# ScalarE issues 30 of the 93 SBUF-to-SBUF copies that SyncE issued, one group later

## The chip, the cores and the metric

One Trainium2 chip, one of its cores. The metric is the device time of one execution in microseconds (us), as the median of several. Engines are named as in the profile: PE (TensorE, with PEld for its weight loads), DVE (VectorE), ACT (ScalarE), POOL (GpSimd) and SP (SyncE), which issues transfers. A row that names `SPq` is SP's queue of instructions.

## What is computed

Two steps over x of 4 batches, 12608 positions and 128 channels:

```python
# 1: a gated long convolution
u = x * v
y = irfft(rfft(u, n=2*S) * rfft(h_filt, n=2*S)[None], n=2*S)[:, :S]   # along the positions
x = x * y
# 2: an expert on the 128 best-scored rows of each batch
scores = x @ w_gate
for b in range(B):
    top_idx = the 128 largest scores of the batch
    xe = x[b, top_idx]
    out[b, top_idx] = xe + sigmoid(scores[b, top_idx])[:, None] * (relu(xe @ w1) @ w2)
```

## The kernel before, in words

The convolution is done by Hartley transforms that are split into a transform over 93 and one over 250 points. The 128 channels are cut into 32 groups of four, so the main loop (line 1249) runs over 128 groups `t`, 32 for each of the 4 batches. In one turn of the loop a new group goes forward: `f_s1` and `dft` on PE, copies on ACT (L483, L344), the product with the filter on DVE (`f_u`, `f_v`, `f_y`: L487 to L501), and a sum and a difference on POOL (`f_sd`: L508, L509). In the same turn the inverse transform `f_i` (L546) runs for a group three turns back, and ACT copies its results out of PSUM (L550 and L551, a pair of copies for two of the four channels). `stage_u` on POOL (L324) multiplies x and v of a group three turns ahead.

PE works in strips of 32 rows, three of which a group needs. The fourth strip is used for every fourth group: the groups with t % 4 = 1, 2, 3 each compute one third of group t - t % 4 in their rows 96 to 127. So three groups of four have a finishing step: POOL adds and subtracts the last columns (`f_c`, L589, two instructions), and then `put(k)` (L559 to L562) moves the third from partitions 96 to 127 of group k to the partitions of group t - t % 4, by a transfer from SBUF to SBUF of 126 KB. There are 93 puts, 84 of them of the whole width. Of the last three groups of batches 0 to 2, ACT copies most of the columns itself (L582) and the put takes the rest.

When all groups of a batch are through (turn 34 of the loop for batch 0, then every 32 turns), `P1.run` does the second inverse step: PE (L636) reads `ay`, the results of all 32 groups, and so has to wait for the puts. DVE multiplies with x (L647), and the scores are summed on ACT (L701). The search for the 128 best rows of a batch runs in small steps in the turns of the next batch.

All transfers of the loop are issued by SP in the order in which the program writes them, and each waits on SP until what it needs is ready: x and v of a group four turns ahead (`load_u`, L318), the stores of the filter's spectrum to DRAM in the first batch (L1305) and its loads in the others (L330), the puts, and the rows of x for `P1` (L611). At the end of a turn stands the list of puts: `due` holds the groups that the turn before finished, and their puts are issued then, one turn after `f_c` was written.

The order on each engine is that of the program (`manual_schedule`). On ACT the end of a turn lies behind the second of the two L483 copies; what follows are the L550 and L551 copies of the next turn, one pair or two, and then L344.

Of the kernel before, what the change touches and what calls it, by code (L numbers as in the profile page):

```python
# [23 lines left out]
NG = 32  # L24
# [214 lines left out]
def hyena_moe(ctx, tc, xg, x2, pos, bw, ww, wg, mw1, mw2, cs, c1, gx, cf, ci, wm, tk, out):  # L239
    nc = tc.nc  # L240
# [73 lines left out]
    def load_u(t):  # L314
        b = t // NG
        if b < B:
            for k, n in enumerate("xv"):
                nc.sync.dma_start(buf(n, t, [NP, XC]), xg[b, :, GC[t], k])  # L318

    def stage_u(t):  # L320
        if t >= B * NG:
            return
        x, v = buf("x", t, [NP, XC]), buf("v", t, [NP, XC])
        nc.gpsimd.tensor_tensor(out=x, in0=x, in1=v, op=ALU.mult)  # L324
# [13 lines left out]
    def dft(t, te, pq):  # L338
        for w in (1, 0):
            for a in range(0, 128, 32):  # L340
                nc.tensor.matmul(pq[w][a:a + 32], lhsT=cf_sb[:, 2 * w + a // NQ, a % NQ:a % NQ + 32],  # L341
                                 rhs=te[:, a // NQ], start=True, stop=True)
        qs = buf("qs", t, [128, HC])
        nc.scalar.copy(out=qs, in_=pq[1])  # L344
        return qs
# [129 lines left out]
    def f_s1(t, dst=None, ps=bank1):  # L475
        u = buf("x", t, [NP, 4, N3])
        te = buf("te", t, [128, 2, 4, N1]) if dst is None else dst
        tps = [view(ps[h], 0, [128, 2, 2, N1]) for h in range(2)]
        for s in range(4):
            for k, c in enumerate(BLK):  # L480
                nc.tensor.matmul(tps[s // 2][c, s % 2], lhsT=u[:, s, c], rhs=c1_sb[:, k], start=True, stop=True)  # L481
        for h in range(2):
            nc.scalar.copy(out=te[:, :, 2 * h:2 * h + 2].rearrange("p e s i -> p s e i"), in_=tps[h])  # L483
        return te.rearrange("p e s i -> p e (s i)")

    def f_u(pq, qs):
        nc.vector.tensor_tensor(out=nat(pq[0]), in0=nat(pq[0]), in1=rev(qs), op=ALU.add)  # L487

    def f_v(pq, qs):
        nc.vector.tensor_tensor(out=nat(pq[1]), in0=rev(pq[0]), in1=nat(qs), op=ALU.subtract)  # L490

    def f_y(t, uv):
        ht = buf("ht", HI[t], [128, 2, HC]) if HS[t] != "hh" else hh[:, GC[t]].rearrange("p e s i -> p e (s i)")
        mt, yz = buf("mt", t, [128, 2, HC]), buf("yz", t, [128, 2, HC])
        for e in (1, 0):
            for o, k in ((mt[:, e], 0), (uv[e], 1)):
                nc.vector.tensor_tensor(out=o, in0=uv[e], in1=ht[:, k], op=ALU.mult)  # L497
        yield yz
        nc.vector.tensor_tensor(out=yz[:, 0], in0=uv[1], in1=mt[:, 0], op=ALU.add)  # L499
        yield yz  # L500
        nc.vector.tensor_tensor(out=yz[:, 1], in0=mt[:, 1], in1=uv[0], op=ALU.subtract)  # L501
        yield yz
# [50 lines left out]
    def parts(t, cols):  # L553
        k = t % 4 - 1
        i, o = ay[96:, GC[t]], ay[32 * k:32 * k + 32, GC[t - t % 4]]
        i, o = (x.rearrange("p (e j) s -> p e (j s)", e=2)[:, :, 4 * cols[0]:4 * cols[1]] for x in (i, o))
        return o, i

    def put(t, *cols):  # L559

        o, i = parts(t, cols or (0, NJ))
        nc.sync.dma_start(o, i)  # L562

    def turn(i):

        g, r = i % NG, i % 4
        if i > DIR:
            u = [(t, s) for t in ((i, DIR) if i == DIR + 1 else (i,)) for s in range(4)]
        elif r == 0:
            u = [(i - 1, s) for s in (1, 2, 3)] if g else []  # L570
        else:
            u = {1: [(i, 0), (i, 1), (i, 2)], 2: [(i - 1, 3), (i, 0), (i, 1)], 3: [(i - 1, 2), (i - 1, 3), (i, 0)]}[r]
            if g == NG - 1:
                u += [(i, s) for s in (1, 2, 3)]
        done = []
        for t, s in u:
            f_i(t, s)
            if s == 3:
                done.append(t)
                if t % NG >= NG - 3 and t < DIR:  # L580
                    o, i = parts(t, (0, JM))
                    nc.scalar.copy(out=o, in_=i)  # L582
        return done

    def f_c(t, ops=(ALU.subtract, ALU.add)):
        a, d = ay[:, GC[t], JM:NJ], ay[:, GC[t], NJ + JM:]
        for op in ops:
            n = NJ - JM - (op == ALU.add)
            nc.gpsimd.tensor_tensor(out=d if op == ALU.subtract else a[:, :n], in0=a[:, :n], in1=stg(t)[:, :n], op=op)  # L589
# [650 lines left out]
    fills = [view(arena, o + a, [128, 512]) for o, w in ((OFF["xa"][0], NX * 8 * D), (XB[0], 8 * D), (OFF["ws"][0], 2 * HW))  # L1240
             for a in range(0, w, 512)]
    fills[-1] = fills[-1][:, :2 * HW - 512]
    due = []

    def small_steps():
        for _ in range(ND):
            bg.hook("d")

    for t in range(NT + LAG):
        g = t % NG  # L1250
        i = t - LAG
        bg.now = t
        done = turn(i) if i >= 0 else []
        if t < NT:
            pq = [bank2[2 - 2 * (t % 2) + e] for e in range(2)]
            spare[0] = [a[:, 512 - NS:] for a in bank1]
            uv[t] = [a[:, :HC] for a in pq]
            qs = dft(t, te.pop(t), uv[t])
            if t == 0:
                rest()  # L1260
            bg.hook("p", 2)
            spare[0] = [pq[0][:, HC:]]
            bg.hook("t", 1)
            spare[0] = [a[:, 512 - NS:] for a in bank1]
            bg.hook("n", 1)
            for k in ((1, 2), (3,), (4,), (5,), ())[t] if t < 5 else (t + 1,):
                if k < NT:
                    te[k] = f_s1(k, ps=banks[6:] if k == 2 else bank1)
            spare[0] = None
            if t != 4:  # L1270
                load_u(t + NU + (t < 4))
            if 0 <= t - 4 < len(fills):
                z = fills[t - 4]
                nc.scalar.activation(out=z, in_=one.to_broadcast([128, z.shape[1]]), func=AF.Copy, scale=0.0)
            o = t - 1 in uv
            if o:
                steps = f_y(t - 1, uv.pop(t - 1))
                y = next(steps)
                next(steps)
            end = t == NT - 1  # L1280
            if end:
                next(steps)
            else:
                small_steps()
            f_v(uv[t], qs)
            if o and not end:
                next(steps)
            if not end:
                bg.hook("e")
            f_u(uv[t], qs)  # L1290
            seam = i >= 0 and i % NG == NG - 1
            now = [k for k in done if seam or end or k % NG == NG - 3]
            done_ = [k for k in done if k not in now]
            for k in now:
                f_c(k)
            if o or t - 1 in ys:
                sd[t - 1] = f_sd(t - 1, y if o else ys.pop(t - 1))
            for k in done_:
                f_c(k, (ALU.subtract,))
            if not seam and t != 4:  # L1300
                stage_u(t + 3 + (t < 4))
            for k in done_:
                f_c(k, (ALU.add,))
            for k in range(4 * (t - 1) // 3, min(4 * t // 3, NG)) if t else ():
                nc.sync.dma_start(hd[:, k], hh[:, k].rearrange("p e s i -> p (e s i)"))  # L1305
            load_h(t + 2)
            for k in due + [k for k in done if k % NG >= NG - 3]:
                put(k, *((JM, NJ) if k % NG >= NG - 3 else ()))
            due = [k for k in done if k % NG < NG - 3]
            for _ in range(0 if end else NE):  # L1310
                bg.hook("e")
            if i >= 0 and i % NG == NG - 1:
                *_, ys[t] = f_y(t, uv.pop(t))
            if t == NT - 1:
                sd[t] = f_last(t, uv.pop(t))
        if t >= NT:
            for k in due:
                put(k)
            due = []
            for k in done:  # L1320
                f_c(k)
        if t == NT:
            bg.drain()
            ex = Experts(picked)
        b = i // NG
        if i >= 0 and i % NG in LA[b]:
            if i % NG == LA[b][0]:
                ph[b] = P1(b)
            k, e = divmod(LA[b].index(i % NG), 2)
            ph[b].load_a(AHEAD[k], e * HB, (e + 1) * HB)  # L1330
        if i % NG == NG - 1 and i >= 0:
            bg.drain("w")
            p1 = ph.pop(b)
            p1.run(ex)
            bg.drain()
            bg = Background(topk_one(b, p1, ex))
# [51 lines left out]
```

## Time and profile before

| | us |
|---|---|
| median of 3 runs | 779.25 |
| lowest, highest of the 3 | 779.14, 783.47 |
| time of the profiled execution | 783.39 |
| its span, first to last instruction | 781.6 |
| PE busy in it | 760.4 |
| DVE, POOL, ACT busy in it | 684.9, 619.5, 572.1 |

The profiled execution is one of those that took some 4 us more than the median. Between its span and its time lie 1.8 us. "Busy" counts the time in which an instruction of that engine ran; transfers that an engine issues are not in it. The waits of an engine are listed by the instruction that waited and by what came last before it went on; "issue" there means that the profile shows nothing that it waited for.

### The profile page before, as it was taken

How to read it: one execution, taken by the hardware profiler on the slowest of the kernel's cores; microseconds unless marked ns; L12 is line 12 of the kernel's file. 1: busy time of each engine (PE TensorE's matmuls, PEld its weight loads, DVE VectorE, ACT ScalarE, POOL GpSimd, SP SyncE). 2: the span in 40 equal slices, each digit the busy share in tenths (PEclk: the TensorE clock that was granted, in tenths of full speed). 3: DMA queues.
4: the chain of work that ended last, by engine and by line, in shares of the span. 5: the costliest groups of instructions: out<-in, count | busy, mean ns of one | idle time of the engine just before them, and what ended most of it. 6: DMA issues, size and time to landing. Idle time of an engine off the chain costs nothing. (4 is left out here: it accounts for less than half of the span.)

```text
span 781.6 us, 37672 instructions
## 1 busy us (share of the span) xinstructions
PE 760.4 (97%) x15191; PEld 560.6 (72%) x15191; DVE 684.9 (88%) x1549; ACT 572.1 (73%) x2286; POOL 619.5 (79%) x704
## 2 busy tenths in 40 slices
PE   8999999999999999999999999999999999999996
PEld 8999767888853677877834777789536778877356
DVE  7468699989989899989899998989998998997992
ACT  0324567756569989886679898986699888975892
POOL 0200189999989799998888899989997998998873
PEclk9999999999999999999999999999999999999999
DMA  9200269999889979999789999999789899995780
GB/s 323 78 28 3 81 226 297 301 305 288 225 276 286 315 242 290 284 280 270 210 261 304 292 264 279 285 269 265 237 275 330 250 275 270 273 272 163 251 298 26
DMA packets 95649, 190.44 MB, mean 244 GB/s; under 512 B 11952, under 2 KB 70256, under 8 KB 95472
## 3 DMA queue, kind: packets, MB, share of 16 engines
q1 hardware_dynamic: 95216, 187.48, 79.8%
q8 instruction: 121, 1.98, 1.1%
q0 software_dynamic: 256, 0.52, 0.2%
q14 instruction: 56, 0.46, 0.2%
HBM read 135.34 MB, written 41.35 MB: 226 GB/s over the span
## 5 line engine op out<-in xcount | busy, mean ns | idle before, releaser
L546 PE MATMUL b<-ci_sb,arena 128*31 128x126 f32 x6096 | 206.6, 270 | 4.4 <-issue 3.8
L341 PE MATMUL c<-arena,cf_sb 128*32 128x372 f32 x2032 | 201.9, 477 | 3.5 <-issue 2.6
L481 PE MATMUL a<-c_sb,arena 128*32 128x186 f32 x4064 | 202.3, 322 | 2.4 <-issue 2.2
L324 POOL TENSOR_TENSOR arena<-arena 128x500 f32<-128x500 f32 x128 | 162.6, 1271 | 46.1 <-DMA arena<-in_xg_dram 23.9
L546 PEld LDWEIGHTS b<-ci_sb,arena 128*31 128x31 f32 x6096 | 184.0, 109 | 12.9 <-issue 6.9
L508 POOL TENSOR_TENSOR arena<-arena 128x372 f32<-128x372 f32 x127 | 116.5, 917 | 80.6 <-DVE arena L501 72.1
L483 ACT COPY arena<-a 128x372 f32<-128x372 f32 x252 | 119.7, 475 | 80.5 <-PE a L481 75.6
L481 PEld LDWEIGHTS a<-c_sb,arena 128*32 128x32 f32 x4064 | 149.0, 109 | 39.0 <-issue 17.7
L701 ACT ACTIVATE arena<-arena 128x128 f32<-128x128 f32 x490 | 143.8, 295 | 13.0 <-DVE arena L691 12.5
L550 ACT COPY big<-b 128x412 f32<-128x412 f32 x192 | 108.3, 565 | 12.4 <-PE b L546 10.5
L509 POOL TENSOR_TENSOR arena<-arena 128x372 f32<-128x372 f32 x127 | 116.1, 914 | 0.0
L341 PEld LDWEIGHTS c<-arena,cf_sb 128*32 128x32 f32 x2032 | 83.1, 109 | 45.9 <-issue 23.0
L589 POOL TENSOR_TENSOR big<-big,arena 128x184 f32<-128x184 f32 x194 | 112.8, 583 | 1.3
L497 DVE TENSOR_TENSOR c<-c,arena 128x372 f32<-128x372 f32 x188 | 102.4, 545 | 0.0
L497 DVE TENSOR_TENSOR arena<-c,arena 128x372 f32<-128x372 f32 x188 | 100.8, 536 | 0.0
L701 ACT ACTIVATION_READ_ACCUMULATOR arena<-arena 128x1 f32 x490 | 91.7, 187 | 0.0
L490 DVE TENSOR_TENSOR c<-c,arena 128x372 f32<-128x372 f32 x128 | 70.3, 550 | 20.5 <-ACT arena L344 14.2
L621 POOL TENSOR_TENSOR arena<-big 96x512 f32<-96x512 f32 x64 | 79.3, 1267 | 0.1
L636 PE MATMUL a<-big,gx_sb 96*64 96x512 f32 (+2 forms) x448 | 75.9, 474 | 1.4 <-DVE arena L647 0.8
L344 ACT COPY arena<-c 128x372 f32<-128x372 f32 x128 | 60.9, 476 | 14.8 <-PE c L341 14.2
L487 DVE TENSOR_TENSOR c<-c,arena 128x372 f32<-128x372 f32 x128 | 70.0, 547 | 0.2
L499 DVE TENSOR_TENSOR arena<-c,arena 128x372 f32<-128x372 f32 x127 | 68.1, 536 | 0.0
(222 smaller groups left out, 1079.8 us busy)
## 6 DMA issues: line engine op xcount, KB each, us to landing
arena<-in_xg_dram SPq DMA_DIRECT2D x256, 250.0 KB, 5.0
arena<-hd SPq DMA_DIRECT2D x178, 186.0 KB, 5.3
out_dram<-arena SPq DMA_DIRECT2D x60, 448.0 KB, 5.6
arena<-in_x_dram SPq DMA_DIRECT2D x36, 448.0 KB, 5.1
hd<-big SPq DMA_DIRECT2D x32, 372.0 KB, 5.1
arena<-in_x_dram SPq DMA_DIRECT2D x48, 224.0 KB, 5.4
big<-big SPq DMA_DIRECT2D x84, 126.0 KB, 5.0
big<-in_pos_dram SPq DMA_DIRECT2D x7, 496.0 KB, 7.0
```

What stands on the lines that cost most here:

```text
L324: nc.gpsimd.tensor_tensor(out=x, in0=x, in1=v, op=ALU.mult)
L341: nc.tensor.matmul(pq[w][a:a + 32], lhsT=cf_sb[:, 2 * w + a // NQ, a % NQ:a % NQ + 32], rhs=te[:, a // NQ], start=True, stop=True)
L481: nc.tensor.matmul(tps[s // 2][c, s % 2], lhsT=u[:, s, c], rhs=c1_sb[:, k], start=True, stop=True)
L483: nc.scalar.copy(out=te[:, :, 2 * h:2 * h + 2].rearrange("p e s i -> p s e i"), in_=tps[h])
L497: nc.vector.tensor_tensor(out=o, in0=uv[e], in1=ht[:, k], op=ALU.mult)
L508: eng.tensor_tensor(out=nat(sd[:, 0]), in0=nat(yz[:, 0]), in1=rev(yz[:, 1]), op=ALU.add)
L509: eng.tensor_tensor(out=nat(sd[:, 1]), in0=rev(yz[:, 0]), in1=nat(yz[:, 1]), op=ALU.subtract)
L546: nc.tensor.matmul(o3[32 * k:32 * k + NT3, s % 2, e * NJ + js.start:e * NJ + js.stop], lhsT=d[:, e, s, c], rhs=ci_sb[:, e, js], start=True ...
L550: nc.scalar.copy(out=ay[:, GC[t], :NJ + JM, ss], in_=o3[:, :, :NJ + JM].rearrange("p s x -> p x s"))
L589: nc.gpsimd.tensor_tensor(out=d if op == ALU.subtract else a[:, :n], in0=a[:, :n], in1=stg(t)[:, :n], op=op)
L621: nc.gpsimd.tensor_tensor(out=cm[:KP, e].rearrange("p j (g s) -> p j g s", s=4), in0=av[0], in1=av[1], op=op)
L701: nc.scalar.activation(out=x, in_=x, func=AF.Copy, accum_out=self.sc[:, j:j + 1])
```

## The change

The puts are divided between two engines. `by_act(t)` is true for every group of the first batch but the last three, and for the 25th to 28th group of the other batches. Since only groups with t % 4 = 1, 2, 3 have a put, these are 21 puts of the first batch and 3 of each other batch, 30 in all. They are issued on ACT's queue instead of SP's. They also wait one more turn in a second list `due2`, so they stand two turns behind their `f_c` and not one. The other 63 puts stay with SP, in their place. Behind the loop's last group (t >= NT) the puts of both lists are issued at once.

```diff
+    def by_act(t):
+        return t < NG - 3 or NG - 8 <= t % NG < NG - 3
+
     def put(t, *cols):
 
         o, i = parts(t, cols or (0, NJ))
-        nc.sync.dma_start(o, i)
+        (nc.scalar if by_act(t) else nc.sync).dma_start(o, i)
...
-    due = []
+    due, due2 = [], []
...
             load_h(t + 2)
-            for k in due + [k for k in done if k % NG >= NG - 3]:
+            for k in due2 + [k for k in due if not by_act(k)] + [k for k in done if k % NG >= NG - 3]:
                 put(k, *((JM, NJ) if k % NG >= NG - 3 else ()))
+            due2 = [k for k in due if by_act(k)]
             due = [k for k in done if k % NG < NG - 3]
...
         if t >= NT:
-            for k in due:
+            for k in due2 + due:
                 put(k)
-            due = []
+            due, due2 = [], []
```

## Rows read from the trace of the kernel before

**Rows 1.** The page: span, and busy time of each engine.

```profile
span 781.6 us, 37672 instructions
PE 760.4 (97%) x15191; PEld 560.6 (72%) x15191; DVE 684.9 (88%) x1549; ACT 572.1 (73%) x2286; POOL 619.5 (79%) x704
```

**Rows 2.** Busy time by stretch, first batch: middle of it and its end.

```profile
core 0: us, PE busy (x) PEld busy (x) DVE busy (x) ACT busy (x) POOL busy (x), PEclk, DMA share, GB/s
...
137.00:164.50 27.50, 27.48 (x682) 23.82 (x677) 26.25 (x57) 18.50 (x49) 27.50 (x34) 1.00 0.94 302
182.00:213.00 31.00, 31.00 (x771) 26.48 (x767) 28.94 (x64) 19.05 (x48) 29.23 (x36) 1.00 0.91 249
```

**Rows 3.** Waits, 106 to 224 us, PE and DVE: total, times, longest.

```profile
PE b L546 <- issue: 1.4, 2, 0.9
...
DVE c L490 <- PE c L341: 4.9, 11, 1.2
DVE c L490 <- ACT arena L344: 2.4, 2, 2.1
```

**Rows 4.** Longest wait of SP's queue, 106 to 224 us.

```profile
SPq L318 <- POOL arena L324: 30.1, 22, 4.7
```

**Rows 5.** Timeline of ACT: L344 of groups 8, 12 and 32 (start, duration).

```profile
117.96 0.47 ACT L344 COPY arena<-c 128x372 f32<-128x372 f32 x1 [0.29 <-PE c L341]
...
133.14 0.47 ACT L344 COPY arena<-c 128x372 f32<-128x372 f32 x1 [0.29 <-PE c L341]
...
213.22 0.47 ACT L344 COPY arena<-c 128x372 f32<-128x372 f32 x1 [0.36 <-PE c L341]
```

**Rows 6.** All puts: duration of the issue in ns, time to landing.

```profile
L562 SPq DMA_DIRECT2D big<-big x93: 507/513/2579, 115.0 to 712.6; - x93
...
DMA to landing us min/median/max: 2.2/4.7/7.2
```

**Rows 7.** The 22 puts from 106 to 224 us.

```profile
DMA to landing us min/median/max: 2.8/5.4/6.5
```

**Rows 8.** Timeline around a turn's end with one pair of copies behind it.

```profile
162.60 0.47 ACT L483 COPY arena<-a 128x372 f32<-128x372 f32 x1 [0.21 <-PE a L481]
162.60 0.62 POOL L589 TENSOR_TENSOR big<-big,arena 128x180 f32<-128x180 f32 x1
...
163.40 0.58 ACT L550 COPY big<-b 128x412 f32<-128x412 f32 x1 [0.33 <-PE b L546]
...
164.46 0.47 ACT L344 COPY arena<-c 128x372 f32<-128x372 f32 x1 [0.34 <-PE c L341]
...
166.40 0.47 ACT L483 COPY arena<-a 128x372 f32<-128x372 f32 x1 [0.21 <-PE a L481]
```

**Rows 9.** Timeline of a turn with two pairs of copies.

```profile
192.08 0.57 ACT L550 COPY big<-b 128x412 f32<-128x412 f32 x1
...
192.97 0.56 ACT L550 COPY big<-b 128x412 f32<-128x412 f32 x1 [0.19 <-PE b L546]
...
193.56 0.47 ACT L344 COPY arena<-c 128x372 f32<-128x372 f32 x1
...
194.26 0.55 DVE L490 TENSOR_TENSOR c<-c,arena 128x372 f32<-128x372 f32 x1
```

**Rows 10.** Timeline: end of the first batch, and end of the last one.

```profile
218.96 0.47 ACT L483 COPY arena<-a 128x372 f32<-128x372 f32 x1 [0.21 <-PE a L481]
...
224.03 1.73 PE L636 MATMUL b<-big,gx_sb 96*64 96x128 f32 x12
...
714.29 0.25 ACT L551 COPY arena<-b 128x92 f32<-128x92 f32 x1
...
715.25 0.55 ACT L550 COPY big<-c 128x412 f32<-128x412 f32 x1 [0.70 <-PE c L546]
...
718.40 2.16 PE L636 MATMUL a<-big,gx_sb 96*64 96x128 f32 x14 [0.63 <-ACT big L550]
```

**Rows 11.** The three puts from 704 to 716 us.

```profile
DMA to landing us min/median/max: 2.2/2.3/3.4
```

## The prediction, made before the changed kernel ran

> **What bounds the kernel now.** I read the page first, then the busy time by stretch, then the waits of each engine, and last the timeline where the changed puts stand. The page shows PE busy for 97% of the span [rows 1], and the stretches of the first batch say the same: in the middle PE has 27.48 us of work in 27.50 and POOL 27.50, near the end PE 31.00 of 31.00 and DVE 28.94 [rows 2]. So a turn of the loop is held by PE, DVE and POOL together, and ACT with 18.50 and 19.05 us has room. The transfer engines are nearly full too (0.94 and 0.91), but that is not what the compute engines wait for: in the waits from 106 to 224 us, PE's longest entry is 1.4 us for nothing that the profile shows, DVE's is 4.9 us for PE, 2.4 us for ACT [rows 3], and neither PE nor POOL has an entry there that names a load. SP's queue does wait a lot, but its longest entry, 30.1 us, is for L324, which has to read an x buffer before the next load may fill it [rows 4]. That is SP running ahead, not SP being late. The pace: groups 8 to 12 took (133.14 - 117.96) / 4 = 3.80 us each, and groups 8 to 32 took 95.26 / 24 = 3.97 [rows 5].
>
> **What SP loses.** 30 issues of about 0.51 us each [rows 6] leave SP: 15.3 us, and with them the waits for `f_c` in front of them. The loads and filter stores behind them can go out earlier. I cost this at nothing, because in the stretch where 21 of them stand no compute engine waits for a load. Its upper bound is what the first batch has over its best pace: 95.26 - 24 * 3.795 = 4.2 us. The lower bound is zero. I take zero: the 1.4 us of PE's waits carry no release by a transfer, and the 4.9 us of DVE's are for PE.
>
> **What ACT gains.** The trace of before has no transfer issued by ACT. The nearest row is the same put on SP: 0.51 us at the median, 2.58 at most [rows 6]; with some 0.1 us between two instructions I take 0.6 us of ACT's time, 18 us for 30. What can be hidden of one put is read from the turn behind it. The put stands behind the second L483 copy, in front of L550. With one pair of copies, ACT sits idle 0.33 us before L550 and 0.34 us before L344 [rows 8]: 0.67 us, more than the put. 20 of the 30 stand so (groups with k % 4 = 1 or 3). With two pairs, which follow the puts of k % 4 = 2 (7 in the first batch and 3 later), ACT is idle only 0.19 us before the second L550, and L344 follows without a gap [rows 9]. L344 then ends at 194.03 and L490, which needs it, starts at 194.26, so another 0.2 us is free. The put sticks out by 0.6 - 0.4 = 0.2 us, and DVE starts that much later, in a stretch where it has 28.94 us of work in 31.00. Ten times 0.2 is 2.0 us at most; where DVE itself lags behind, as early in the batch, nothing. I take half: **+1.0 us**. If there were no cover at all it would be 30 * 0.6 = 18 us.
>
> What is queued behind a waiting put on ACT are L550, L551 (they free PSUM for `f_i`), L344 (DVE waits for it) and the next L483 (PE's `dft` waits for it). So it matters whether the put has to wait. Its source is ready when POOL's second L589 ends, here at 162.60 + 0.62 = 163.22. ACT reaches the end of the next turn, where SP's list has that put, at 162.60 + 0.47 = 163.07, which would be 0.15 us too early, and the end of the turn after that, where the new list has it, at 166.40 + 0.47 = 166.87 [rows 8]. With the added turn the put finds its data ready 3.65 us before. Cost zero; the cover is gone only if POOL falls back a whole turn.
>
> **What becomes later.** Nothing in the loop reads what a put moves before `P1`, so for 17 or so of the first batch's puts a turn's delay is free. It counts for group 27 of a batch, the last one moved. At the end of the first batch ACT is through with L483 at 218.96 + 0.47 = 219.43, and L636 starts at 224.03: 4.60 us for issue and landing [rows 10]. The ends of batches 1 and 2 repeat the pattern, with 4.6 us both. In the last batch, two puts stand behind the four copies of the first group after the loop: ACT is free at 714.54, idle for 0.70 us until 715.25, and would issue until about 715.75 [rows 10]. L550 comes 0.5 us late there, but the four copies that follow each wait 0.17 us for PE or more, and PE writes four separate banks, so nearly all of it is made up. The second put starts at about 715.15 and has 718.40 - 715.15 = 3.25 us to land.
>
> Landing time is the uncertain part. Puts of the last stretch landed in 2.2 to 3.4 us [rows 11], those of the whole run in 4.7 at the median [rows 6], those of the first batch in 5.4, at most 6.5 [rows 7]. By 2.3 us nothing is late; by 4.7 the three ends are 0.1 us late and the last 1.45, together 1.75; by 6.5 it is 3 * 1.9 + 3.25 = 8.95. The puts in question are closest to the row of the last stretch for the last batch, and for the other ends to the median. I take +0.3 for the first three ends and nothing for the last, **+0.3 us**.
>
> The Trainium skill ("DMA: Bandwidth & Descriptors", section "Queues, rings and completion order") says that SP and ACT each own a row of rings and that a transfer engine takes turns between the rows it has work for. By that rule a put on ACT's row would not stand behind SP's loads, its landing would be near the lowest row, and this term would be zero instead of 0.3; no run so far shows it, as all transfers of the loop share one queue.
>
> **The sum.** 0 + 1.0 + 0.3 = +1.3 us on the span of 781.6, so 782.9 for an execution like the profiled one (784.7 with the 1.8 us around it). On the median of 779.25, which lies 4.1 us under the profiled execution, the same addition gives **780.5 us**.
>
> **The rivals.**
>
> - *SP's relief pays.* Earlier loads and filter stores let the turns of the first batch run at their best pace. For it speaks that 95.26 us are 4.2 more than 24 best turns; against it that no engine's wait there names a load. Time: 779.25 - 4.2 = 775.0. It would still be under 1%.
> - *The puts reach `P1` late.* They land as the first batch's puts did, in 5.4 us: 3 * 0.8 + 2.15 = 4.55, with ACT's 1.0 some 784.8; at 6.5 us each, 779.25 + 8.95 + 1.0 = 789.2. Against it: landings near the batch ends are shorter.
> - *ACT's issues stand on the path* (the other side). Place: between L483 and L550. Price: 0.6 us each without cover, 18 us, 797.3; more if an issue stalls as the longest on SP did, 2.58 us. It decides from 7.8 / 30 = 0.26 us that isn't hidden of each put. For it speaks that in two-pair turns ACT has no gap before L344; against it ACT's idle third in rows 2 and that two puts of three find 0.67 us.
> - *The change doesn't do what it says*: ACT stands waiting for POOL's L589, because POOL lags by more than a turn in the full stretch. Price per put up to the missing time; at 0.3 us for 21 puts 6.3 us, 786.6 with the 1.0. Against it the 3.65 us.
>
> **How the numbers follow.** The forecast, with 778 to 783 of its own, has 0.62; SP's relief 0.20; late landing 0.09; ACT on the path 0.06; ACT waiting for POOL 0.03. The range has to leave out no more than 0.2: from SP's relief at its full size, 775, to late landing at its middle size, 785. A measurement of this kernel can tell about 1%, 7.8 us, from no change. Faster by more would need nearly twice what the first batch has over its pace: 0.03. Slower by more comes from ACT on the path (0.05), late landing at its longest (0.02) and waiting (0.01): 0.08. The rest, 0.89, is the same.
>
> **What would show it.** Right: 63 puts on SP, 30 on ACT, each near 0.5 us long; the L344 intervals of the first batch near 3.97 us on average; L490's waits for L344 up by a few times 0.2 us; L636 starting as long after the last L483 as now. Wrong: ACT issues of 1 us and more, or L550 and L344 waiting with PE's L546 gaps behind them (ACT on the path); L636 released by a transfer at a batch's end (late landing); or groups 8 to 32 in under 93 us (SP's relief).

## The result and the profile after

| | before | after |
|---|---|---|
| median, us | 780.81 (6 runs) | 788.10 (6 runs) |
| lowest, highest | 779.14, 783.47 | 786.31, 789.40 |
| profiled execution: time, span | 783.39, 781.6 | 788.94, 787.2 |

The ratio is 1.0082, with a 95% interval from 1.0053 to 1.0111: some 6.4 us slower on the 780.81 of these runs (the medians differ by 7.3). The prediction was 780.5 us, 1.3 us more than the 779.25 that it started from, in a range from 775 to 785. All ratios in this text are to the kernel before, run on the same chip.

Line numbers from the put on are 3 higher after: the put is L565, the loads of x L614, the second inverse step L639. First the page: span and busy times (for [rows 1]), two of its costliest groups (busy time and mean ns, then the idle time before them and what ended most of it), and the puts by issuing engine (KB each, median us to landing).

```profile
span 787.2 us, 37667 instructions
PE 758.3 (96%) x15191; PEld 550.0 (70%) x15191; DVE 683.5 (87%) x1549; ACT 569.9 (72%) x2286; POOL 619.8 (79%) x704
...
L550 ACT COPY big<-b 128x412 f32<-128x412 f32 x192 | 107.6, 562 | 34.3 <-POOL arena L324 11.1
...
L490 DVE TENSOR_TENSOR c<-c,arena 128x372 f32<-128x372 f32 x128 | 71.2, 556 | 29.7 <-ACT arena L344 26.6
...
big<-big SPq DMA_DIRECT2D x54, 126.0 KB, 5.3
big<-big ACTq DMA_DIRECT2D x30, 126.0 KB, 4.2
```

The same two groups on the page of before:

```profile
L550 ACT COPY big<-b 128x412 f32<-128x412 f32 x192 | 108.3, 565 | 12.4 <-PE b L546 10.5
...
L490 DVE TENSOR_TENSOR c<-c,arena 128x372 f32<-128x372 f32 x128 | 70.3, 550 | 20.5 <-ACT arena L344 14.2
```

The busy times of PE, DVE, ACT and POOL are those of before within 2.2 us, so no work was added; engines stand longer, ACT ahead of L550 for 34.3 us instead of 12.4. Who stands is in the waits from 106 to 224 us, the stretch of [rows 3] (total, times, longest):

```profile
DVE c L490 <- ACT arena L344: 11.3, 7, 4.5
ACT big L550 <- POOL arena L324: 10.3, 5, 4.3
PE b L546 <- ACT arena L551: 3.7, 2, 2.1
```

DVE's wait for ACT was 2.4 us in [rows 3] and is 11.3; PE's L546 waits 3.7 us for ACT, an entry that the same view of before does not have. So ACT became late, and it did so ahead of L550, the copy right behind the put. The names after the arrow of ACT's entries are only what happened to end last before it (L550 uses nothing of POOL's L324). The puts themselves look harmless (durations in ns, then the landing of those on ACT):

```profile
L565 ACTq DMA_DIRECT2D big<-big x30: 514/514/716, 116.3 to 719.1; - x30
...
DMA to landing us min/median/max: 2.4/4.2/4.9
```

The time is lost ahead of a put's row, not in it. The timeline of the end of the first batch (start, duration, in brackets the idle time before), to be held against [rows 10]:

```profile
213.68 0.45 SPq L614 DMA_DIRECT2D arena<-in_x_dram  x1
...
215.75 0.47 ACT L483 COPY arena<-a 128x372 f32<-128x372 f32 x1 [0.21 <-PE b L546]
...
219.81 0.51 ACTq L565 DMA_DIRECT2D big<-big  x1
...
220.37 0.52 ACT L550 COPY big<-b 128x412 f32<-128x412 f32 x1 [4.14 <-POOL arena L324]
...
221.07 1.06 PE L546 MATMUL b<-ci_sb,arena 128*31 128x126 f32 x32 [1.62 <-ACT arena L551]
...
222.71 0.55 DVE L490 TENSOR_TENSOR c<-c,arena 128x372 f32<-128x372 f32 x1 [4.50 <-ACT arena L344]
...
228.25 1.73 PE L639 MATMUL b<-big,gx_sb 96*64 96x128 f32 x12
```

ACT ends L483 at 216.22 and stands until 219.81. Then come the put, L550, L551 and L344; PE stood 1.62 us for L551, DVE 4.50 us for L344. The second inverse step starts at 228.25, 4.2 us later than the 224.03 of [rows 10].

**What the put waits for.** The list of waits in the built program has two entries for such a put: POOL, and one of eight counters that count landings. Around group 26:

```
place  issued by   line             counts on   waits for
153    SP          L614 (x)         counter 1   counter 1 at 304
...
161    ACT         L565 (group 26)  counter 1   POOL, counter 1 at 320
```

Every transfer of the loop, on SP or ACT, takes the next of the eight counters, in one order over both queues, and first waits until the transfer that used it last, as a rule the one eight places earlier, has landed. So ACT stands for a transfer that SP issued, at group 26 for a load of x. From the trace's records of these counters (all five of these are transfers of SP; that of group 15 is a store of the spectrum, the others are loads):

| put of group | POOL ready | transfer eight places earlier landed | put starts | idle ahead of L550 |
|---|---|---|---|---|
| 2 | 119.07 | 121.05 | 121.12 | 0.74 |
| 15 | 169.05 | 172.65 | 172.72 | 2.39 |
| 17 | 176.42 | 180.06 | 180.13 | 2.18 |
| 18 | 180.43 | 186.35 | 186.43 | 4.29 |
| 26 | 213.72 | 219.74 | 219.81 | 4.14 |

The idle time ahead of L550 takes in some 0.56 us for the put itself; the wait alone is 3.59 us at group 26 (from 216.22 to 219.81). In 12 of the 30 puts, 10 of them in the first batch, the start follows the counter by 0.07 to 0.08 us. For the others the counter had been there before, or its records are incomplete. POOL was ready 1.2 to 6.1 us ahead of every put of the first batch. The load of x issued at 213.68 was on its way for 6.06 us.

The Trainium skill ("DMA: Bandwidth & Descriptors", section "Why a DMA increments its semaphore by 16 and not by 1") says why a program must wait so: when two transfers in flight count on one semaphore, its value no longer tells that the first has landed. The counter's steps of 16 (304, 320) agree. The Trainium skill's "Perfetto Trace Analysis", section "DMA Instruction — HWDGE (DVE, Sync)", has the wait done by the issuing engine's sequencer, and the recorded start behind it; the rows agree: the put of group 26 has a row of 0.51 us, and the 3.59 us before it are in no row.

### The profile page after: what moved, and what is told of

Same layout as the page of the kernel before. It is cut to its first block, busy times and chain, and to the rows that moved or that the text cites. A ratio compares the mean times of both kernels' runs of the same rounds, so it can differ in the third digit from the quotient of the medians.

```text
span 787.2 us, 37667 instructions
## 1 busy us (share of the span) xinstructions
PE 758.3 (96%) x15191; PEld 550.0 (70%) x15191; DVE 683.5 (87%) x1549; ACT 569.9 (72%) x2286; POOL 619.8 (79%) x704
## 5 line engine op out<-in xcount | busy, mean ns | idle before, releaser
L546 PE MATMUL b<-ci_sb,arena 128*31 128x126 f32 x6096 | 202.5, 270 | 12.9 <-issue 6.3
L324 POOL TENSOR_TENSOR arena<-arena 128x500 f32<-128x500 f32 x128 | 162.6, 1270 | 45.6 <-DMA arena<-in_xg_dram 45.3
L481 PE MATMUL a<-c_sb,arena 128*32 128x186 f32 x4064 | 196.3, 321 | 1.6 <-issue 1.5
L341 PE MATMUL c<-arena,cf_sb 128*32 128x372 f32 x2032 | 195.5, 477 | 2.1 <-ACT arena L483 0.8
L546 PEld LDWEIGHTS b<-ci_sb,arena 128*31 128x31 f32 x6096 | 179.7, 109 | 23.9 <-issue 9.3
L508 POOL TENSOR_TENSOR arena<-arena 128x372 f32<-128x372 f32 x127 | 116.4, 916 | 81.6 <-DVE arena L501 73.3
L481 PEld LDWEIGHTS a<-c_sb,arena 128*32 128x32 f32 x4064 | 140.0, 109 | 44.1 <-issue 20.2
L483 ACT COPY arena<-a 128x372 f32<-128x372 f32 x252 | 120.4, 478 | 69.1 <-PE a L481 62.6
L550 ACT COPY big<-b 128x412 f32<-128x412 f32 x192 | 107.6, 562 | 34.3 <-POOL arena L324 11.1
L341 PEld LDWEIGHTS c<-arena,cf_sb 128*32 128x32 f32 x2032 | 75.7, 109 | 46.2 <-issue 22.3
L497 DVE TENSOR_TENSOR c<-c,arena 128x372 f32<-128x372 f32 x188 | 103.7, 552 | 0.0
L497 DVE TENSOR_TENSOR arena<-c,arena 128x372 f32<-128x372 f32 x188 | 102.1, 543 | 0.0
L490 DVE TENSOR_TENSOR c<-c,arena 128x372 f32<-128x372 f32 x128 | 71.2, 556 | 29.7 <-ACT arena L344 26.6
L639 PE MATMUL a<-big,gx_sb 96*64 96x512 f32 (+2 forms) x448 | 76.1, 474 | 1.4 <-DVE arena L650 0.8
L487 DVE TENSOR_TENSOR c<-c,arena 128x372 f32<-128x372 f32 x128 | 71.0, 555 | 0.2
L499 DVE TENSOR_TENSOR arena<-c,arena 128x372 f32<-128x372 f32 x127 | 69.5, 547 | 0.0
L344 ACT COPY arena<-c 128x372 f32<-128x372 f32 x128 | 61.5, 481 | 10.2 <-PE c L341 9.4
```

The source lines that it names most:

```text
L508: eng.tensor_tensor(out=nat(sd[:, 0]), in0=nat(yz[:, 0]), in1=rev(yz[:, 1]), op=ALU.add)
L546: nc.tensor.matmul(o3[32 * k:32 * k + NT3, s % 2, e * NJ + js.start:e * NJ + js.stop], lhsT=d[:, e, s, c], rhs=ci_sb[:, e, js], start=True ...
L550: nc.scalar.copy(out=ay[:, GC[t], :NJ + JM, ss], in_=o3[:, :, :NJ + JM].rearrange("p s x -> p x s"))
```

## The experiments

In the texts on record theory A is: the puts on ACT wait for a transfer eight places earlier, and ACT's copies behind them. B: 30 issues of 0.51 us are not hidden. C: puts land late at the second inverse step. `by_act` chooses the puts that go to ACT and that are a turn later. The table has the runs that the argument rests on; the others (e6 to e11) stand with their texts.

| kernel | on ACT | ratio | interval |
|---|---|---|---|
| the change | 30 | 1.0082 | 1.0053 to 1.0111 |
| the change again (e17) | 30 | 1.0107 | 1.0069 to 1.0146 |
| later on SP (e2) | 0 | 1.0136 | 1.0065 to 1.0207 |
| first batch only (e3) | 21 | 1.0064 | 1.0025 to 1.0103 |
| later batches only (e4) | 9 | 1.0007 | 0.9976 to 1.0037 |
| earlier in the turn (e5) | 30 | 1.0066 | 1.0033 to 1.0099 |
| not later (e12) | 30 | 1.0119 | 1.0084 to 1.0154 |
| later on SP, groups 1 to 23 (e13) | 0 | 0.9995 | 0.9969 to 1.0021 |
| groups 1 to 23 (e14) | 18 | 1.0006 | 0.9973 to 1.0039 |
| groups 25 to 27 of batch 0 (e15) | 3 | 1.0053 | 1.0018 to 1.0088 |
| all but those three (e16) | 27 | 1.0015 | 0.9980 to 1.0051 |

**The two halves of the change.** First the turn's delay alone:

```diff
-        (nc.scalar if by_act(t) else nc.sync).dma_start(o, i)
+        nc.sync.dma_start(o, i)
```

> The two-turn delay alone: the same 30 puts one turn later, but all 93 issued by SyncE. Theory A (ScalarE's puts wait for one of eight completion counters that all queued transfers share, that is until the transfer eight places earlier has landed, and hold up ScalarE's copies): 780 to 782 us, ratio 0.998 to 1.002, since SyncE takes the waits and no compute engine does. Theory B (the half microsecond of ScalarE's time for each of 30 issues, not hidden): 780 to 782 too. Theory C (the later puts land late at the second inverse step): about 788, ratio 1.008.

Measured: 787.18 (4 runs) against 777.86, 1.0136. Both A and B missed; C's 1.008 lies within the interval. The trace shows a cost at the same place, the end of the batch. SP issues in the program's order, so the late puts stand behind loads: the put of group 27 is issued at 220.89 and lands at 226.92, and PE stands for it. The profile names a load of the filter (`hd`) as the releaser, but in the built program this L639 waits for landings of puts alone. Then the granted clock is down (third number from the right of a stretch):

```profile
227.27 2.52 PE L639 MATMUL b<-big,gx_sb 96*64 96x128 f32 x12 [3.52 <-DMA arena<-hd]
```

```profile
core 0: us, PE busy (x) PEld busy (x) DVE busy (x) ACT busy (x) POOL busy (x), PEclk, DMA share, GB/s
222.00:226.00 4.00, 1.75 (x40) 1.02 (x32) 2.56 (x6) 2.20 (x6) 3.84 (x6) 1.00 1.01 304
226.00:230.00 4.00, 2.73 (x14) 1.69 (x16) 1.77 (x5) 0.27 (x1) 3.80 (x5) 0.76 0.75 210
230.00:234.00 4.00, 4.00 (x18) 1.72 (x16) 1.80 (x3) 0.22 (x1) 2.07 (x2) 0.81 0.52 169
```

A wait of 3.3 us for a transfer stands at the end of the third batch too. That this is the whole cost was tried by delaying only puts that nobody waits for soon (`by_act` is `t < NG - 7`, all on SP):

> All puts on SyncE; those of the groups 1 to 23 alone are one turn later, those of 25 to 27 and of the other batches as before. The deferral of all 30 on SyncE cost 1.4 (0.7 to 2.1) per cent, and its trace shows the second inverse step waiting 3.5 us for data in the first and the third batch, at a clock that then falls. If that wait is the whole cost, this one is within 2 us of the kernel before. If the deferral costs SyncE in the turns themselves, 3 us or more slower.

Measured: 777.83 against 779.04, 0.9995. So the delay costs nothing that can be measured within the batch; on SP it costs at the batch's end. In the change, with the last puts on ACT, no L639 waits for them. The other half, ACT without the delay:

```diff
-            for k in due2 + [k for k in due if not by_act(k)] + [k for k in done if k % NG >= NG - 3]:
+            for k in due + [k for k in done if k % NG >= NG - 3]:
...
-            due2 = [k for k in due if by_act(k)]
```

> The 30 puts on ScalarE, but not one turn later: the move alone. With the deferral GpSimd's last adds were ready 0.9 us (median) before the puts were issued in the first batch and at worst under 0.1 us, so one turn of some 4 us earlier ScalarE waits for GpSimd some 1 to 3 us at most of the puts, on top of the landings. Theory A: 6 to 20 us slower than the change. Theory B: as the change, within 2 us.

Measured: 786.93 against 779.04, 1.0119, 9.3 us by the ratio. That is 1 to 3 us over the two measurements of the change, whose intervals overlap with this one: A's "6 to 20 us slower than the change" missed, and B's "as the change, within 2 us" can't be told from it. The 0.9 us in the text is wrong, the median lead of POOL in the first batch of the change is 2.6. But ACT did stand: in the trace 0.6 to 1.9 us ahead of L550 at most puts. L344 of the groups 7 to 32 was 0.7 to 2.5 us late, no later with each stall; it went to 5.2 us only at the end of the batch, behind an idle time of 4.04 us ahead of L550 at 220.83. That is the first sign that stalls don't add up, and the loss comes without the delay too.

**Which puts.** Only `by_act` differs in these two.

> ScalarE issues only the 21 puts of the first batch, one turn later; SyncE issues the other 72. Theory A: in the trace after the change 12 of the waits that ended with such a counter stand in the first batch and they hold ScalarE for some 17 us, the 9 others for under 2 us; so nearly the whole loss, 786 to 788, ratio 1.006 to 1.009. Theory B: 21/30 of the loss, 785.3. Theory C: three of the four batch ends as before, about 782 to 783.

> ScalarE issues only the 9 puts of the 25th to 28th groups of batches 2 to 4. Theory A: 781 to 782, ratio 1.000 to 1.002, with at most two waits of 0.2 to 1 us at the end of batch 2. Theory B: 9/30 of the loss, 782.7. Theory C: three of the four ends late, about 786.

Measured 782.33 and 777.36 against 777.86: 1.0064 and 1.0007. A hit with both. C missed the second, so the loss does not come from the ends of the later batches. B is not excluded by this pair, since 21/30 and 9/30 of the change's 1.0082 are 1.0057 and 1.0025, within the two intervals. (In the text, 12 is the count of the whole execution; 10 of these waits stand in the first batch.) Where in the turn they stand matters little (the puts written ahead of the L483 copies, behind L344):

> The same 30 puts on ScalarE, but ahead of the two L483 copies of the turn, where ScalarE sits idle 0.79 us for TensorE in most turns. Theory B: the issue is hidden there, so most of the loss goes: 781 to 783. Theory A: ScalarE comes to the put 1.3 us earlier, and the wait for the transfer eight places back, landing some 6 us after its issue, stays: L483 instead of L550 is held up; 785 to 791, ratio 1.005 to 1.013, with idle times of 2 us and more before L483. Theory C: 788 as with the change.

Measured: 782.54 against 777.86, 1.0066 (1.0033 to 1.0099). A hit, with idle times of up to 3.02 us ahead of L483; B, 1.003 at most, missed; C can't be told apart here.

**The number of transfers.** If the eight counters are the cause, one more transfer a turn must lengthen the waits, though ACT's queue is not touched. Into both kernels went:

```diff
+    scr = cp.tile([128, NG], F32, name="scr")
...
+            if 4 <= t < NG:
+                nc.sync.dma_start(scr[:, t:t + 1], one)
```

> The changed kernel with one transfer of 512 B more a turn on SP in the turns 4 to 31, put ahead of the puts. Read it against the next kernel. Theory A: eight places back is now one transfer later in each of these turns, mostly a store of a spectrum or a load of x that was issued within the last turn or so; ScalarE's stalls in the first batch grow from 15.7 us to 25 or more and the gap to the next kernel from 6.4 us to 10 or more. Theories B and C: the gap stays at 5 to 8 us, because nothing is changed on ScalarE's queue or behind the puts.

> The kernel before with the same 28 small transfers; the partner of the last one. SP has some 0.5 us more to issue a turn and one more wait: by all theories 0 to 4 us slower than the kernel before.

Measured: 794.48 and 783.02, a gap of 11.5 us (ratios 1.0177 and 1.0031). A hit with both its numbers, the gap and the stalls below. The two intervals leave the gap uncertain by some 5 us, so it is the stalls, not the gap, that speak against B and C. The waits of the first, in the same stretch as above (L491 and L551 are here what L490 and L550 were):

```profile
DVE c L491 <- ACT arena L345: 14.5, 10, 4.1
ACT big L551 <- PE a L482: 8.9, 3, 3.4
ACT big L551 <- POOL arena L509: 7.8, 5, 2.4
```

ACT's idle times over 1 us ahead of that copy, up to 230 us, are now 14 with 33.4 us together; in the change they are 7 with 17.7 (the text's 15.7 was summed wrongly). The opposite was tried with fewer, larger transfers (not shown: the two halves of an early load of x are joined too):

```diff
-            for e in range(2):
-                nc.sync.dma_start(ht[:, e], hd[:, GC[t], e * HC:(e + 1) * HC])
+            nc.sync.dma_start(ht.rearrange("p e s -> p (e s)"), hd[:, GC[t]])
...
-                nc.sync.dma_start(hd[:, k], hh[:, k].rearrange("p e s i -> p (e s i)"))
+                if k % 2:
+                    nc.sync.dma_start(hd[:, k - 1:k + 1], hh[:, k - 1:k + 1].rearrange("p g e s i -> p g (e s i)"))
...
```

> The changed kernel with fewer SP transfers (spectra stored in pairs, each group's filter read back in one transfer, the two halves of an early load joined). The bytes are the same. Read it against the next kernel, which has the same merges without the change. Theory A (a ScalarE put stands until the transfer eight places before it in the order of all queued transfers has landed): with fewer transfers a turn, eight places reach further back, to a transfer that landed earlier, so the stalls of ScalarE over 1 us ahead of its copy of the inverse product sink from seven in the first batch (15.7 us) to at most three, and the gap to the next kernel sinks from 6.4 us to under 3. Theory B (the 0.51 us of issue, 30 times): the gap stays at 5 to 7 us. Theory C (puts land late at the second inverse step): the gap stays.

> The kernel before with the same merges; the partner of the last one. By all theories within 4 us of the kernel before: SP has fewer issues, but it isn't the bound. If SP's issues did hold the first batch up, 3 to 6 us faster.

Measured: 800.99 (791.42 to 806.39, 4 runs, too scattered for a ratio) and 788.55 (1.0112, 1.0080 to 1.0145). The four runs lie 3 to 18 us above the partner, so the gap, which A had under 3 us, can't be told. In the trace ACT's stalls behind puts are gone up to 221 us, as A has it, but one of 2.8 us stands at the end of the batch, and PE lost time in another way (waits from 106 to 230 us; L549 and L545 are L550 and L546 here):

```profile
ACT big L549 <- POOL arena L508: 2.8, 1, 2.8
PE b L545 <- issue: 4.2, 5, 2.2
```

The merging made both kernels slower, so the times of this pair test nothing; the stalls within the batch speak for A. PE's waits for "issue" from 402 to 550 us are 5.2 and 7.7 us here, against 2.0 before; why larger transfers do that stays open.

**Which stalls count.** In the trace of the change the lateness of L344 falls back after nearly every stall and stays only after the last. Six puts that stood in the change and in e3 alike, or the last of them alone (group 26), went back to SP, still late (shown is the second; the first has `t not in (2, 6, 15, 17, 18, 26)`):

```diff
-        (nc.scalar if by_act(t) else nc.sync).dma_start(o, i)
+        (nc.scalar if by_act(t) and t != 26 else nc.sync).dma_start(o, i)
```

> The changed kernel, with the six puts of the first batch (groups 2, 6, 15, 17, 18 and 26) behind which ScalarE's copy of the inverse product stood 0.7 to 4.9 us in both kernels with the puts on ScalarE given back to SyncE, still one turn late. The other 24 keep their place and the transfer that they wait for. Theory A (ScalarE stands until the transfer eight places earlier has landed): at most one stall over 1 us is left on ScalarE in the first batch, and of the 7.3 us that the change costs at most 2.5 are left. Theory B (0.51 us of issue each): 24/30 of it, 5.8 us. Theory C (late landing at the second inverse step, which the fourth kernel back showed for SyncE): no better than the change, 7 us or more.

> The changed kernel with one put alone, that of group 26, given back to SyncE. In the trace of the change ScalarE stands 4.14 us behind it at 220.37, and the lateness of the first batch steps from about 0.7 to 4.7 us there and stays; the lateness of the earlier stalls (up to 2.2 us at group 25) shrank again. Theory A with that reading: 3 to 4 of the 7.3 us are gone, and the second inverse step of the first batch starts within 1.5 us of the kernel before. Theory B: 29/30 are left, 7.1 us. If the early stalls add up after all, 5 to 6 us are left.

Measured: 785.23 (1.0060, 1.0028 to 1.0092) and 790.07 (1.0108, 1.0054 to 1.0163), the latter not better than the change. The interval of the first, 2.2 to 7.2 us, holds A's 2.5, B's 5.8 and C's 7 alike, but A's "at most one stall" missed; the second is a miss for A. The other puts did not all keep the transfer that they wait for: a put that moves to SP takes another place in the order of the counters. In the first's trace four stalls over 1 us ahead of L550 are left in the batch (11.3 us together), two of them (3.32 us at group 5, 3.76 at group 19) behind puts whose copies stood some 0.6 us in the change, and the last, 2.84 us at 222.69, behind the put of group 27. In the second's trace (795.99 us, the longest of its five executions) the stall of group 26 is gone and L344 of group 33 is on time, but now the put of group 27 stands, and the transfer eight places before it is the put of 26, which SP issued at 218.22:

```profile
222.34 0.52 ACTq L565 DMA_DIRECT2D big<-big  x1
...
222.89 0.53 ACT L550 COPY big<-b 128x412 f32<-128x412 f32 x1 [3.50 <-DMA big<-big]
```

So the stall was handed on. The clean division leaves the last three puts of the first batch as they were before, or moves only them (`by_act` is `t < NG - 7`; `NG - 8 <= t < NG - 3`; and the change without the latter). Each put keeps the transfer that it waits for.

> The 18 puts of the groups 1 to 23 of the first batch on ScalarE, one turn later; all the others (25 to 27 of the first batch and the later batches) as before the change. Theory A' (a stall counts only if nothing later in the batch takes it up, so the last one counts): at most 2.5 us slower than the kernel before, though ScalarE's stalls up to 190 us are still there. Theory A (all stalls add up): 4 to 6 us slower. Theory B (0.51 us of issue each, 18 of the 30): 18/30 of the change's 6 to 7 us, 4 us slower.

> The three puts of the groups 25, 26 and 27 of the first batch alone on ScalarE, one turn later; the other 90 as before. Each waits for the landing of the same kind of transfer as in the change: a gathered load, and twice a load of x. Theory A': 3 to 6 us slower than the kernel before, with one stall of 3 to 5 us ahead of ScalarE's copy of the inverse product near 219 us and nothing over 1 us before it. Theory A: 2 to 3 us slower. Theory B: 3/30, 0.7 us slower.

> The change without those three: 27 puts on ScalarE, one turn later, the groups 25 to 27 of the first batch as before. Theory A': within 3 us of the kernel before. Theory A: 4 to 6 us slower. Theory B: 27/30 of the change's, 6 us slower.

> The change itself, on the same chip as the last three: by every theory 5 to 9 us slower than the kernel before, as measured (7.3 us).

Measured against 780.76: 781.20, 783.04, 782.41 and 786.37, ratios 1.0006, 1.0053, 1.0015, 1.0107. Eighteen puts on ACT cost nothing that can be measured, nor do 27 (1.2 us by the ratio, with an interval that holds zero), and three cost 4 us by the ratio (1.4 to 6.9 by its interval; the medians differ by 2.3). Taking these three out of the change gives back 7 us by the ratios. A' hit all three. A and B missed e14, and B also e15 and e16; A's numbers for these two lie in their intervals or at their ends. In the trace of e16 the stall of group 18 is as long as in the change, PE and DVE wait for it, and the second inverse step still starts at 223.39, earlier than in [rows 10]:

```profile
185.73 0.51 ACTq L565 DMA_DIRECT2D big<-big  x1
186.29 0.52 ACT L550 COPY big<-b 128x412 f32<-128x412 f32 x1 [4.49 <-POOL arena L324]
...
186.99 1.27 PE L546 MATMUL b<-ci_sb,arena 128*31 128x126 f32 x39 [2.03 <-ACT arena L551]
...
223.39 1.78 PE L639 MATMUL b<-big,gx_sb 96*64 96x128 f32 x12
```

With the three alone (e15) ACT has no idle time over 1 us ahead of L550 before 217 us. Then it has two, 2.07 us at 217.07 and 2.62 at 222.93, where one of 3 to 5 was expected. The puts of groups 26 and 27 start 0.08 us after the counter there, for which they stood with POOL ready 4.9 and 6.7 us earlier:

```profile
222.38 0.51 ACTq L565 DMA_DIRECT2D big<-big  x1
...
223.65 1.90 PE L546 MATMUL b<-ci_sb,arena 128*31 128x126 f32 x32 [3.35 <-ACT arena L551]
...
229.83 1.73 PE L639 MATMUL b<-big,gx_sb 96*64 96x128 f32 x12
```

The lateness against the trace of before, in us from the start of each span: L344 of four groups (0 is the first), and the start of the second inverse step.

| | group 24 | 25 | 26 | 32 | second step |
|---|---|---|---|---|---|
| change | -0.7 | 2.2 | 0.6 | 0.6 | 4.2 |
| change again | -0.9 | 0.7 | -0.9 | -0.3 | 2.6 |
| all but the three | -1.6 | 1.5 | -0.1 | -0.7 | -0.6 |
| the three alone | -2.3 | -2.3 | -2.5 | -0.6 | 5.8 |

These traces differ by 2 us and more without the change: that of e15 moves no put before group 25 and is 2.3 us ahead there, and that of the change again is 0.6 us ahead from the first group on. So only steps within a row and the large values of its last column count. Within the batch a stall of 3 to 4 us leaves up to 3 us more lateness at one group (25) and half of that or less at the next. Why is read from the steps of before: from group 20 on L344 follows L344 by 3.80 us at best, POOL's L508 follows L508 by 4.02 us at the median. PE, ACT and DVE can run faster than POOL and make up what they lost, as long as POOL sets the pace; that reading is not shown by a run of its own. At the end of the batch no turn is left to make it up in; the second step is 2.6 to 5.8 us late with the three puts on ACT, and 0.6 us early without them.

None of these kernels is faster than the kernel before.

## Why the prediction was wrong, step by step

**The step that failed** is "What is queued behind a waiting put". It put down correctly who stands behind it (L550, L551, L344, the next L483) and asked only whether POOL's L589 is done: "the put finds its data ready 3.65 us before. Cost zero". On POOL it was right: ready 1.2 to 6.1 us ahead. But a put has a second thing to wait for, the landing of a transfer issued shortly before, and that comes last where a load takes 6.06 us as above. The step was mis-sized at 0; it costs 4 us (e15, 1.0053) to 7 us (e17 less e16) for the three puts at the end of the first batch and nothing that can be measured for the others (e14, e4).

The trace of before held the sign. These are waits of its SP queue over the whole execution, which the prediction did not use:

```profile
SPq L562 <- DMA arena<-in_xg_dram: 3.3, 6, 0.8
...
SPq L562 <- DMA arena<-hd: 2.8, 6, 1.0
```

A put reads neither x and v (`in_xg_dram`) nor the filter (`hd`), and yet it went on when such a load had landed, 12 times. On SP only transfers stand behind such a wait, and SP runs ahead [rows 4]; on ACT copies stand behind it.

**Point by point.**

- *What bounds the kernel*, PE, DVE and POOL at the pace of [rows 5]. Not contradicted: with 18 and 27 puts on ACT the time stays (e14, e16). What it left out is that the end of a batch is another stage, where a delay of ACT isn't made up.
- *What SP loses: 0.* Held: e4, e14 and e16 take 9 to 27 issues off SP and are not faster; the rival of SP's relief is out with them.
- *What ACT gains: +1.0 us for issues that stick out.* Within what e14 (1.0006) and e4 (1.0007) can tell. The rival *ACT's issues stand on the path* (18 us) is out with the same two.
- *Late landing: +0.3.* No L639 waits for a put in the trace after, so the term was small, as said. The 21 puts of the first batch land in 4.4 us at the median on ACT's queue (3.5 at the least), against 5.4 for those of [rows 7]. The Trainium skill ("DMA: Bandwidth & Descriptors", section "Queues, rings and completion order") has SP and ACT each own a row of rings. The prediction took from it that the landings would come near the lowest row. They are shorter, but not by that much, and no run here shows that the row is the reason. Without ACT's queue the rival would have been right: e2's L639 waits 3.52 us.
- *The change doesn't do what it says: ACT stands waiting.* This rival had 0.03 and was right about who stands and who waits for it, and wrong about what for. Its 786.6 lies near the measured time, but by another sum.
- *What would show it wrong* named L550 and L344 waiting with PE's L546 gaps behind them, and that is what the trace after shows. It laid them to issues of 1 us and more, which don't exist: the longest is 0.72 us.

**What stays open.** e14, e15 and e4 together make 1.0066, the change 1.0082 and, again, 1.0107. The intervals overlap; whether 1 to 3 us come from the parts together is not settled. In e15's trace the granted clock fell, as the last section shows, and in that of the change it did not, so part of e15's 4 us may be the clock's. In the profiled execution of the change another 2 us of lateness appear at the end of the third batch, with gaps of PE that the profile calls "issue". The moved puts of that batch are not needed for them: e3 moves none there and has such gaps too (0.67 us ahead of L546 at 550.04, 0.95 at 549.52 in the change), and the change again has none. Why they come stays open.

## What to carry to other kernels

Before a transfer is moved to an engine that computes, ask for everything that it waits for, also for transfers that it has no data in common with: the queue's waits in the old trace name them. Then price the engine's stall by where it falls: within a batch of this loop a stall of 4 us cost nothing that could be measured, and at the end of the batch 3 of 30 puts carried most of the loss. An experiment that hands a wait to another transfer has not removed it.

## What the runs showed of the hardware

A transfer issued by ACT can stand for one issued by SP, though each has its own queue: 12 puts started 0.07 to 0.08 us after another transfer's counter. That the eight counters are shared in one order is how this program was built; no run here shows that the chip asks for it.

In e15 a pause of PE cost twice. PE was busy for 2.15 us of the stretch from 218 to 222 and then paused, 3.35 us in all, until the row at 223.65. The granted clock of the next two stretches was 0.54 and 0.61 on average (0.5 is the lower level, 1.2 GHz); the same 32 matmuls that took 1.06 us in the change (at 221.07) took 1.90.

```profile
218.00:222.00 4.00, 2.15 (x70) 1.65 (x61) 2.53 (x6) 2.28 (x6) 2.40 (x4) 1.00 1.03 272
222.00:226.00 4.00, 2.35 (x40) 1.84 (x44) 1.18 (x3) 2.42 (x6) 2.71 (x4) 0.54 0.86 259
226.00:230.00 4.00, 4.00 (x52) 1.88 (x46) 1.84 (x5) 1.97 (x5) 1.85 (x3) 0.61 0.34 96
```

In the change PE's longest pause there was 1.62 us, and the clock stayed at 1.00. So the fall isn't what made the change slower. The traces of e2 and e11 have it at the same place (0.76 and 0.81, 0.85 and 0.72). How much it adds to the times of e2, e11 and e15 was not tested: the seven runs of e15 with a mean clock of 0.999 or 1.0 still go from 778.80 to 787.86 us.
